# Pooled-key attention feeding a rotated token mix: scores scaled in the copied keys, the row maximum stored with its sign turned, and a newly drawn order of work

## The chip, the cores and the metric

The kernel runs on one core of one Trainium2 chip. The metric is device microseconds of one execution; before and after are compared by the medians of several runs. The engines are called PE (matrix multiplication; PEld is its weight load), DVE (vector), ACT (scalar, activation functions), POOL (GpSimd) and SP (the queue that issues most transfers).

## The reference, cut to what matters

```
def _attn_ref(q, k, v):                      # q, k, v: 8 x 8 x 576 x 64
    scale = 1.0 / np.sqrt(D)                 # D = 64
    k_p = k.reshape(B, H, Sp, pool, D).mean(axis=3)      # pool = 8, Sp = 72
    v_p = v.reshape(B, H, Sp, pool, D).mean(axis=3)
    scores = scale * np.matmul(q, k_p.transpose(0, 1, 3, 2))
    scores = scores - np.max(scores, axis=-1, keepdims=True)
    attn = np.exp(scores)
    attn = attn / (np.sum(attn, axis=-1, keepdims=True) + 1e-09)
    return np.matmul(attn, v_p)

def _moe_ref(x, w_theta, w_tok_r, w_tok_i, w_ch):        # x: 8 x 576 x 512
    theta = x @ w_theta
    zr = x * np.cos(theta)
    zi = x * np.sin(theta)
    y = np.einsum('ts,bsd->btd', w_tok_r, zr) + np.einsum('ts,bsd->btd', w_tok_i, zi)
    u = x + y
    return u + np.maximum(u @ w_ch, 0.0)
```

The attention output, with its heads side by side, is the x of the second part. The four weights arrive as 64-bit numbers and are turned into pairs of 32-bit words in the kernel.

## The kernel before, in words

The work goes over eight batches b. For each batch there are streams of small steps, and every stream is a Python generator that issues the instructions of one step each time it is called:

- k, v and Q load keys, values and queries (SP). K sums eight neighbouring keys (the pooling) and puts them, transposed on PE, into the block tile kpT; V does the sums of the values.
- S{b}.{m} is the softmax of one of five token tiles (the function soften): four groups of matmuls of kpT with the queries into PSUM (line 648), the maximum of 72 scores for each of eight heads on DVE (tile mx, line 682), eight exponentials with a sum each on ACT (line 691, tile e_eps), one instruction that adds the small constant to the sums (line 695), the reciprocal on DVE (line 707), and two steps that multiply by it (lines 712 to 723). For batches from 2 on, a DVE transpose into G follows (line 732), and E moves blocks of G by 16 transfers into eraw. Between the maximum and the exponentials one short ACT instruction (line 687) multiplies the maximum by minus the score scale, because the exponential takes scale times score plus a bias.
- X multiplies the weights by the pooled values, T rotates by cosine and sine (pt, line 829; g, lines 835 to 858), Z and Y split z into two parts whose sum keeps the accuracy of 32 bits, and M is the token mix (py, line 972), U splits u, and F is the final product (pf, line 1075). The weights come by h (theta), w and W (token weights, turned on PE) and c (channel weights); P and R make sums of the turned token weights.

The order of all this is written out by hand of a program: SCHEDULE is a text of 2166 words. A word such as S1.2a calls the next step of stream S1.2 and says that a step that can run on several engines runs on ACT (a), DVE (v) or POOL (g). All engines' queues follow this one order; SP's transfers too. A step's engine and its place are thus fixed when the kernel is built, and an engine that waits for one instruction holds up all that stands behind it in its queue.

In batch 0 the maximum, the multiplication and the exponentials are three words; from batch 1 on the maximum and the multiplication are one word, so the short ACT instruction stands in ACT's queue at the place of the maximum. The score scale is 1/(8 * sqrt(64)) = 1/64 in every softmax (the factor 1/8 is the mean over eight keys).

Of the kernel before, what the change touches and what calls it, by code (L numbers as in the profile page):

```python
# [82 lines left out]
T3.3 T3.3 F2.3.1 F2.0.1 S4.3 F1.2.1 F2.1.1 F2.2.1 Z3.0a F2.1.0 v5.1 Z3.0v Z3.0g Z3.0g S4.4 V5.1g F2.0.0 F2.0.1 F2.0.1
Z3.0v M3.0 M3.0 F2.2.1 Z3.0a Z3.0v Q5.1 M3.0 F2.1.1 Q5.1 Z3.0g S4.4 S4.4a F2.0.1 Q5.1 M3.0 M3.0 Z3.0g Z3.0v S4.4v
Z3.0a X4.0 F2.2.1 Y3.0g M3.0 S4.4 M3.0 Z3.0v F2.3.1 F2.1.1 Z3.0g M3.0 F2.2.0 Z3.0a Y3.0v Z3.0g F2.3.0 M3.0 F2.3.1
Z3.0v Z3.1v Y3.0g X4.0a M3.0 Z3.0g M3.0 X4.0a S5.2 Z3.1v Z3.1a k6.2 M3.1 k6.0 M3.0 S5.4 Z3.0g T4.0a M3.0 E4.2 S5.2
S5.2 E4.2 S5.3 Y3.1g Z3.1v T4.0v Z3.1v F2.2.1 Y3.1g K6.0v S5.2 Z3.1a M3.1 S5.2a S5.4 Y3.1v M3.1 E4.2 E4.2 Z3.1v Z3.1g
M3.1 S5.3 U3.0.0a T4.0 M3.1 S5.2v U3.1.0g Z3.1g k6.1 M3.0 Z3.1v Z3.1a Z3.1v M3.1 M3.1 S5.2 S5.3 S5.3 Y3.1v T4.0 T4.0
# [58 lines left out]
def tile_attn_moe(  # L147
# [485 lines left out]
    def soften(b, m):  # L633
# [47 lines left out]
        for scv, mxv, _, _ in views:  # L681
            nc.vector.tensor_reduce(mxv, scv, AX.X, ALU.max)  # L682
# [583 lines left out]
```

## Time and profile before

| what | value |
|---|---|
| median of 3 runs | 562.45 us (561.65 to 563.61) |
| the profiled execution | 562.28 us |
| span of its profile | 560.5 us |
| granted clock of PE, mean | 0.985 |
| busy: PE, PEld, DVE, ACT, POOL | 524.5, 477.6, 475.1, 408.5, 326.8 us |

The span runs from the first to the last instruction; 1.8 us of the profiled execution's time lie around it. Matmuls overlap in their pipeline, so that the busy time of PE is more than the time for which it holds up the next matmul.

### The profile page before, as it was taken

Reading aid. Unit: us, or ns where it says so; the run is one execution under the profiler, and the core shown is the slowest. Engines: PE = TensorE matmul, PEld = TensorE weight load, DVE = VectorE, ACT = ScalarE, POOL = GpSimd, SP = SyncE. Lnnn points to the kernel's source line nnn. Section 1 sums busy time; section 2 is a strip of 40 time slices with the busy share of each in tenths; the row PEclk is TensorE's granted clock in tenths of the full one; section 3 lists DMA queues with packets and bytes.
Section 4 is the critical chain, followed back from the end, with each engine's and each line's share of the span. In section 5 each row is a group of like instructions: output and inputs, shape, how many; then the busy total and the mean of one; then the engine's idle time right before and its main releaser. Section 6 shows DMA issues by size and latency. Waiting matters only on the chain.

```text
span 560.5 us, 11892 instructions
## 1 busy us (share of the span) xinstructions
PE 524.5 (94%) x3927; PEld 477.6 (85%) x3927; DVE 475.1 (85%) x913; ACT 408.5 (73%) x1318; POOL 326.8 (58%) x458
## 2 busy tenths in 40 slices
PE   6687679999999999999999999999999999999996
PEld 6575468898998899889989888989999888889996
DVE  3996999987999888998899979897997879977864
ACT  2896899897898789889757767876987758644211
POOL 4543574365596767765486647567767546534451
PEclk9989987999999999999999999999999999999999
DMA  9999410273667867554845657345436461220126
GB/s 264 319 221 229 109 38 1 69 149 93 118 114 129 131 151 131 125 107 80 146 96 93 103 100 129 71 79 117 70 57 102 87 112 22 34 37 1 23 44 105
DMA packets 232493, 58.92 MB, mean 105 GB/s; under 512 B 218864, under 2 KB 220528, under 8 KB 232432
## 3 DMA queue, kind: packets, MB, share of 16 engines
q1 hardware_dynamic: 227456, 57.52, 51.3%
q10 hardware_dynamic: 4976, 0.64, 0.8%
q8 instruction: 31, 0.51, 0.4%
q14 instruction: 30, 0.25, 0.2%
HBM read 38.86 MB, written 9.44 MB: 86 GB/s over the span
## 4 chain that ended last, share of the span: by engine, by line
PE 57%; DVE 16%; ACT 12%; DMA 7%; issue 3%; POOL 2%; SPq 2%; DVEq 0%; ACTq 0%; POOLq 0%
PE py L972 22%; PE pf L1075 11%; PE pt L829 11%; ACT e_eps L691 5%; PE s L648 4%; PE pv L778 2%; DMA qst<-in_q_dram 2%; PE px L843 2%; DVE mx L682 1%; DMA kprst<-in_k_dram 1%; DMA kpst<-in_k_dram 1%; PE pv L785 1%; DVE xT L988 1%; PE kpp L542 1%; ACT en L712 1%
## 5 line engine op out<-in xcount | busy, mean ns | idle before, releaser
L972 PE MATMUL py<-WTh,zs 128*128 128x288 f32 x576 | 96.1, 292 | 0.2 <-DVE g L837 0.2
L691 ACT ACTIVATE e_eps<-s,mx 128x72 f32<-128x72 f32 (+1 forms) x304 | 92.7, 328 | 2.8 <-DVE en L716 1.5
L972 PEld LDWEIGHTS py<-WTh,zs 128*128 128x128 f32 x576 | 79.8, 189 | 5.4 <-issue 2.5
L691 ACT ACTIVATION_READ_ACCUMULATOR e_eps<-s,mx 128x1 f32 (+1 forms) x304 | 64.9, 214 | 0.0
L988 DVE TENSOR_TENSOR xT<-py,xT 128x288 f32<-128x288 f32 x106 | 46.8, 446 | 18.9 <-PE py L972 18.9
L890 DVE TENSOR_TENSOR zs<-z,zs 128x512 fp32r<-128x512 f32 x80 | 60.9, 767 | 1.6 <-POOL zs L208 0.6
L191 POOL TENSOR_TENSOR zs<-z,zs 128x256 fp32r<-128x256 f32 x52 | 41.6, 823 | 24.1 <-ACT zs L206 12.8
L972 PE MATMUL py<-WSh,zs 128*128 128x288 f32 x336 | 54.1, 290 | 1.3 <-DVE xT L988 0.6
L206 ACT CAST zs<-z 128x512 fp32r<-128x512 f32 x56 | 34.0, 615 | 25.9 <-POOL z L191 12.0
L648 PE MATMUL s<-kpT,qT 128*128 128x144 f32 (+1 forms) x320 | 48.6, 298 | 3.3 <-DVE qT L208 1.4
L712 ACT ACTIVATE en<-e_eps,ri 128x64 f32<-128x64 f32 (+1 forms) x176 | 44.6, 337 | 6.0 <-DVE G L732 3.1
L972 PEld LDWEIGHTS py<-WSh,zs 128*128 128x128 f32 x336 | 46.0, 189 | 3.0 <-DVE zs L890 1.1
L648 PEld LDWEIGHTS s<-kpT,qT 128*128 128x128 f32 (+1 forms) x320 | 42.5, 185 | 6.7 <-DVE qT L208 1.7
L191 POOL TENSOR_TENSOR z<-z 128x256 f32<-128x256 f32 (+1 forms) x58 | 42.2, 747 | 9.9 <-DVE zs L890 7.2
L972 PE MATMUL py<-WTl,zs 128*128 128x288 f32 x288 | 47.1, 286 | 0.0
L1075 PE MATMUL pf<-uh,chh 128*128 128x288 f32 x256 | 44.0, 293 | 1.8 <-DVE uh L208 1.4
L829 PE MATMUL pt<-th,xh 128*128 128x512 f32 x148 | 41.9, 407 | 1.6 <-DVE zo L864 0.6
L191 POOL TENSOR_TENSOR ul<-xT,uh 128x288 fp32r<-128x288 f32 x37 | 31.5, 861 | 20.0 <-ACT uh L206 14.1
L835 ACT ACTIVATE g<-pt,c_magic 128x512 f32<-128x512 f32 x35 | 23.9, 683 | 25.1 <-PE pt L829 13.2
L1075 PE MATMUL pf<-ul,chh 128*128 128x288 f32 x256 | 41.9, 286 | 0.0
L1075 PE MATMUL pf<-uh,chl 128*128 128x288 f32 x256 | 41.8, 286 | 0.0
L972 PEld LDWEIGHTS py<-WTl,zs 128*128 128x128 f32 x288 | 40.1, 189 | 0.0
(238 smaller groups left out, 1445.3 us busy)
## 6 DMA issues: line engine op xcount, KB each, us to landing
out_dram<-R SPq DMA_DIRECT2D x112, 72.0 KB
kpst<-in_k_dram SPq DMA_DIRECT2D x15, 512.0 KB
vpst<-in_v_dram SPq DMA_DIRECT2D x28, 256.0 KB
qsst<-in_q_dram SPq DMA_DIRECT2D x96, 72.0 KB
eraw<-G SPq DMA_DIRECT2D x96, 60.0 KB
eraw<-G SPq DMA_DIRECT2D x96, 40.0 KB
WTh_st<-in_moe_w_theta_dram SPq DMA_DIRECT2D x4, 512.0 KB
wcraw<-in_moe_w_ch_dram SPq DMA_DIRECT2D x4, 512.0 KB
```

Source lines behind the costliest of these rows:

```text
L191: nc.gpsimd.tensor_tensor(out[:, r], a[:, r], b[:, r], op)
L206: nc.scalar.copy(out, src)
L648: nc.tensor.matmul(scs[c // 2][:n, 2 * SP * (c % 2) : 2 * SP * (c % 2 + 1)], qT[:, c, t0 : t0 + n], kpT[:, c, :], start=True, stop=True,)
L691: nc.scalar.activation(e[:n, x], scs[j][:n, SP * y : SP * y + SP], AF.Exp, bias=mx[:n, x : x + 1], scale=scale, accum_out=sm[:n, x : x + 1],)
L712: nc.scalar.activation(en[:n, GM * h : GM * h + GM], e[:n, h, 0:GM], AF.Copy, scale=ri[:n, h : h + 1])
L778: nc.tensor.matmul(pvs[j][to : to + 64, c, :gn], vm[r, 2 * j + c, :], ev[r, 2 * j + c, :gn], start=True, stop=False,)
L829: nc.tensor.matmul(as_written(pt), l[:, c, :], by_turns(r[:, c, :]), start=i == 0, stop=i == 11)
L835: nc.scalar.activation(halves(g), in_order(pt), AF.Identity, bias=c_magic)
L890: ENG[pick()].tensor_tensor(dst[:, 1], src, f32(dst[:, 0]), ALU.subtract)
L972: nc.tensor.matmul(as_written(to[:, 0 : S // 2]), left(l, kk), by_turns(weights(what, kk)[r]), start=start and i == 0, stop=stop and i == ...
L988: nc.vector.tensor_tensor(halves(u), in_order(py[:, 0 : S // 2]), halves(u), ALU.add)
L1075: nc.tensor.matmul(as_written(pv[:, :n]), l[:, kk, o], by_turns(uhl[r][:, kk]), start=i == 0, stop=i == 11,)
```

## The change: what it does

The pooled keys are multiplied by 1/64 while they are copied into kpT (four copies and one remainder for each batch), by an activation on ACT or a multiplication on DVE in place of a plain copy. The scores in PSUM are then scaled already. The maximum is stored with its sign turned by the reducing instruction itself, so that it is the bias of the exponential as it is. The ACT instruction of line 687 is gone (40 times, 5 words of batch 0 with it), and the exponentials take no scale. The order is drawn anew: SCHEDULE has 2161 words, nearly all streams' words stand at other places (half of them within 6 places of their old one, the farthest 130), and 308 words name another engine.

```diff
+    def scaled(e, out, src, by):
+        if e == "a":
+            nc.scalar.activation(out, src, AF.Copy, scale=by)
+        else:
+            ENG[e].tensor_scalar(out, src, by, None, ALU.mult)
+
+    SCORE = 1.0 / (POOL * math.sqrt(D))
...
-        copy(e, blocks[0:64, :, 0::3], heads[:, 0::2].rearrange("p (j c) g -> p j c g", c=2))
+        scaled(e, blocks[0:64, :, 0::3], heads[:, 0::2].rearrange("p (j c) g -> p j c g", c=2), SCORE)
...
-        copy(pick(), kpT[64:128, 3, GR:SP], pr[0:64, 0:64])
+        scaled(pick(), kpT[64:128, 3, GR:SP], pr[0:64, 0:64], SCORE)
...
-            nc.vector.tensor_reduce(mxv, scv, AX.X, ALU.max)
+            nc.vector.tensor_reduce(mxv, scv, AX.X, ALU.max, negate=True)
         if b == 0:
             yield
         sm = work([P, 8], F32, "sm", f"sm{b}_{m}", bufs=2)
         if b < SUMS_ON_ACT:
-            nc.scalar.mul(mx[:n], mx[:n], -scale)
-            yield
+            if b:
+                yield
             for x in range(8):
                 j, y = at(x)
                 nc.scalar.activation(
                     e[:n, x], scs[j][:n, SP * y : SP * y + SP], AF.Exp,
-                    bias=mx[:n, x : x + 1], scale=scale, accum_out=sm[:n, x : x + 1],
+                    bias=mx[:n, x : x + 1], accum_out=sm[:n, x : x + 1],
                 )
```

Of the order, the words that load in the first part, before and after:

```
before: k1.0 Q0.3 h3 w1.1 h2 Q0.4 w1.0 Q1.1 k1.1 Q1.0 v0.2 w2.0 v0.1 v1.0 Q1.2 v0.0 k1.2 ... w3.0 Q1.4 c0 k2.2 w4.0 c1
after:  h3 Q0.3 k1.0 Q0.4 h2 Q1.1 w1.0 w1.1 v0.2 k1.1 Q1.0 w2.0 v0.1 v1.0 v0.0 Q1.2 k1.2 ... w3.0 Q1.4 c0 w4.0 k2.2 c1
```

## Rows read from the trace of the kernel before

**Rows 1.** The page, busy time, share of the span and instructions of each engine.
```profile
PE 524.5 (94%) x3927; PEld 477.6 (85%) x3927; DVE 475.1 (85%) x913; ACT 408.5 (73%) x1318; POOL 326.8 (58%) x458
```

**Rows 2.** Stages: length, busy PE, PEld, DVE, ACT, POOL; clock, DMA share, GB/s.
```profile
20.00:55.00 35.00, 25.75 (x181) 21.22 (x179) 29.86 (x59) 30.11 (x120) 15.43 (x17) 0.90 1.05 252
55.00:86.00 31.00, 20.53 (x126) 16.25 (x127) 28.60 (x46) 27.24 (x62) 19.70 (x22) 0.90 0.24 68
...
100.00:460.00 360.00, 355.38 (x2693) 326.10 (x2692) 316.07 (x604) 288.79 (x990) 232.74 (x342) 1.00 0.58 107
```

**Rows 3.** The chain that ended last: start, length, what; four kinds of matmul.
```profile
417.50 1.47 PE py L972 x12
418.97 0.98 PE s L648 x8
421.78 2.59 PE pt L829 x12
444.09 4.41 PE pf L1075 x36
```

**Rows 4.** PE alone in one stage, for tiles py, pf, pt, s in turn.
```profile
100.00:460.00 360.00, 151.16 (x1126) 1.00 0.58 107
...
100.00:460.00 360.00, 76.00 (x574) 1.00 0.58 107
...
100.00:460.00 360.00, 75.71 (x324) 1.00 0.58 107
...
100.00:460.00 360.00, 36.92 (x256) 1.00 0.58 107
```

**Rows 5.** Groups of instructions: the maximum, its multiplication, the copies into kpT.
```profile
L682 DVE TENSOR_REDUCE mx<-s 128x8 f32<-128x576 f32 (+2 forms) x42 | 29.8, 714 | 1.9 <-PE s L648 1.9
...
L687 ACT ACTIVATE mx<-mx 128x8 f32<-128x8 f32 (+1 forms) x40 | 8.2, 205 | 17.1 <-DVE mx L682 16.9
L707 DVE RECIPROCAL ri<-sm 128x8 f32<-128x8 f32 (+1 forms) x40 | 7.6, 190 | 3.8 <-ACT sm L695 3.3
...
L206 ACT COPY kpT<-pk 64x288 f32<-64x288 f32 (+3 forms) x24 | 5.0, 258 | 0.1
```

**Rows 6.** The chain around the multiplication of the maximum.
```profile
134.16 0.22 ACT mx L687
```

**Rows 7.** Waits: who waited for whom, total us, times, longest.
```profile
ACT mx L687 <- DVE mx L682: 16.9, 12, 2.4
```

**Rows 8.** ACT by shape: a scaled copy and a plain one out of PSUM, smaller ones.
```profile
L712 ACT ACTIVATE en<-e_eps,ri 128x64 f32<-128x64 f32 x152 | 38.5, 337 | 4.7 <-DVE G L732 3.1 <-DVE ri L707 1.0 <-PE per L746 0.6
...
L791 ACT ACTIVATE xT<-pv 128x512 f32<-128x512 f32 x13 | 7.5, 592 | 6.2 <-DVE R L1112 3.4 <-PE pv L785 2.7
...
L206 ACT COPY eraw<-pe 128x512 f32<-128x512 f32 x7 | 4.1, 579 | 1.1 <-PE pv L785 0.7 <-PE pe L741 0.4
...
L206 ACT COPY kpT<-pkr 64x64 f32<-64x64 f32 x7 | 1.5, 209 | 0.2
```

**Rows 9.** Groups: the final product with PE's waits before it, and key sums on DVE.
```profile
L1075 PE MATMUL pf<-uh,chh 128*128 128x288 f32 x256 | 44.0, 293 | 1.8 <-DVE uh L208 1.4 <-DVE g L837 0.4
...
L466 DVE TENSOR_TENSOR kpst<-kpst 128x512 f32<-128x512 f32 (+1 forms) x16 | 9.5, 593 | 0.5 <-DMA kpst<-in_k_dram 0.2
```

**Rows 10.** The chain in the start: two transfers, and where PE's long run begins.
```profile
36.63 7.90 DMA kprst<-in_k_dram
46.50 8.84 DMA qst<-in_q_dram
85.77 4.99 PE pt L829 x12
```

**Rows 11.** SP in time: the transfers of c0, k2.2 and w4.0.
```profile
47.97 0.33 SPq L368 DMA_DIRECT2D wcraw<-in_moe_w_ch_dram  x1
55.94 0.49 SPq L494 DMA_DIRECT2D kprst<-in_k_dram  x1
56.48 0.59 SPq L404 DMA_DIRECT2D WSh_st<-in_moe_w_tok_r_dram  x1
```

More of the change, by code (lines that the diff above doesn't have):

```diff
@@ new lines @@
+w0.0 Q0.0a h1 h0 K0 h1v K0a K0.2v w0.1v K0 K0v Q0.1 h3 S0.0 w0.1a Q0.2 Q0.3 w0.1v k1.0 Q0.2a h1 w0.1 h0a S0.0 w0.1
+Q0.4 Q0.1v S0.1 h0v h0v h3v S0.0 h2 h0 Q1.1 Q0.3 Q0.4 S0.1 h3a Q0.3a S0.2 S0.0 w1.0 h3a h0 K1.0v S0.1 h0v Q0.4a w1.1
+v0.2 S0.0v S0.0g h0 h3 k1.1 S0.0 S0.0a S0.3 h2v S0.0 S0.2 S0.1 W0 h2v S0.2 h2v h2 h3 S0.1v h2 S0.4 S0.0v S0.3 S0.2
+w1.0v w1.1a S0.1v w1.0a Q1.0 w1.1a h3v w1.0a h2v Q1.1 Q1.1a K1.1v h2 w2.0 S0.1 S0.2v Q1.0 w1.0 S0.3 w1.1a h3 w1.0
+w2.0a S0.2g Q1.0v v0.1 S0.4 W0a w1.1 V0.2 w1.1 v1.0 S0.1v K1 S0.1 W0 V0.1 W1 V1.0v S0.3 v0.0 S0.2 Q1.2 S0.4 W0 w2.0v
@@ new lines @@
+S0.3g W1a V0.0 W0v S0.4 S0.3g K1a W0 S0.1v W1 k1.2 w2.0a Q1.3 w2.1 V0a W1 W1v V0 Q1.2 W1 w2.1a Q1.3 w2.1a w3.1 v1.1
+X0.0 X0.0a S0.2a w2.0 Q1.3v Q1.2v w3.1a X0.0v S0.3 S0.2 S0.2a S0.4v S0.3a T0.0v S0.4v K1.2g w3.0 w2.1a S0.4 T0.0v
+T0.1a V1.1v S0.3 Q1.4 T0.0 T0.1v c0 S0.4a S0.4 w3.1a w4.0 w3.0a c0v w2.1 S0.3a S0.4a K1 T0.0 w3.0v w2.0 w3.0a c0a T0.0
+w2.1 X0.2 Q1.4 T0.0 K1v c0a c0 T0.0 w3.1v T0.0a w3.0 X0.2v k2.2 X0.2v T0.1 T0.0 T0.1 W2 c1 T0.2a T0.3a K2.2g w4.0a
+w4.0a w3.0 w3.1 W2v S1.0 w4.0v S1.0 W2 c0 T0.1 w3.1 T0.1 v1.2 w4.0 W3 c0g T0.0 S1.0 c0g T0.2v W2 W3v T0.0 T0.1 T0.1a
@@ new lines @@
+Z1.0v U0.3.1a U0.3.1v Z1.0v E2.0 F0.1.1 k3.1 Z1.0a Z1.0v T1.4 F0.1.1 F0.1.1 S2.4 E2.0 T1.4 T1.4 F0.0.1 Z1.0g S2.2
+K3.1v T1.4 S2.2 V3.2g M1.0 F0.0.0 E2.0 S2.3 R2g T1.4 F0.1.1 E2.0 F0.0.1 F0.3.0 F0.2.1 T1.4 Z1.0a F0.3.1 M1.0 S2.2a
+S2.3 F0.2.1 Z1.0g Q3.0 S2.4 Y1.0g F0.3.1 S2.2g F0.0.0 K3 R2g Y1.0g F0.0.1 M1.0 S2.3 M1.0 S2.2 Z1.0g R2a S2.3 Z1.0g
+Z1.0v K3v Y1.0g R2g Q3.1 M1.0 F0.0.1 Z1.0a S2.3a M1.0 Z1.0v S2.3g M1.0 V2g S2.4 Q3.1 Z1.0v R3v F0.3.1 R3v S2.3 R3a
+S2.4 Z1.0g F0.3.1 F0.2.0 M1.0 F0.2.1 M1.0 Z1.0g X2.0 K3 S2.4a Z1.0v R3g S2.4v M1.0 K3a Y1.0a Z1.1g Z1.1g Z1.1a S2.4
@@ new lines @@
+U1.1.0g T2.1 T2.1 U1.0.0g T2.2a S3.0 K4.0g U1.1.0v T2.1 F1.3.0 k4.1 F1.1.0 E3.2 T2.2v M1.1 F0.2.1 V4.2g E3.2 T2.1a
+T2.2 T2.1 F1.3.0 F1.0.0 F1.1.0 T2.1 S3.0 T2.1 T2.2 F1.1.0 Q4.0 K4.1g S3.1 F1.2.0 T2.2 U1.0.1v T2.2 T2.2 T2.2a T2.3g
+F1.2.0 F1.0.0 U1.3.1v U1.0.1v T2.2 T2.2 U1.2.1a U1.3.1g T2.2 T2.3 U1.1.1a T2.3 U1.1.1v S3.0 K4 U1.2.1g T2.3 F1.1.1
+S3.0g v4.0 F1.1.1 Q4.1 F1.0.0 T2.3 F1.1.1 T2.3 V3g T2.3a S3.0g T2.3 T2.3 S3.0 S3.1 F1.0.1 F1.0.1 T2.3 F1.3.1 Q4.1
+Z2.0v F1.0.1 Z2.0v Z2.0v F1.2.1 F1.1.1 K4a F1.2.1 M2.0 Q4.1 F1.0.1 S3.1 V4.0g k5.2 K4 K4a Z2.0v X3.2 F1.2.0 F1.2.1
@@ new lines @@
+U2.0.1a U2.1.1a F2.2.0 T3.3 U2.0.1v T3.3 U2.2.1a U2.1.1v U2.3.1g T3.3 K5a Q5.1 T3.3a U2.2.1v U2.3.1v F2.3.1 T3.3
+F2.1.1 F2.0.0 T3.3 T3.3 Z3.0a F2.1.1 F2.1.1 F2.0.1 Z3.0v Z3.0a F1.3.1 M3.0 V5.1g k6.2 F2.3.1 Z3.0v Z3.0v M3.0 M3.0
+Z3.0v F2.0.1 F2.1.1 Z3.0g F2.2.1 k6.0 F2.0.1 Z3.0g S4.4 Z3.0g F2.0.0 S4.4 S4.3 M3.0 Y3.0v M3.0 F2.2.1 F2.2.0 F2.2.1
+S4.4a Z3.0v X4.0 S4.4g M3.0 Z3.0a S4.4 F2.0.1 F2.3.0 M3.0 Z3.0v Z3.0g Z3.0a F2.3.1 M3.0 M3.0 Q5.1 Z3.0g X4.0a X4.0a
+M3.0 Y3.0a E4.2 U3.0.0a Z3.0g M3.0 Z3.1g S5.2 Z3.0a S5.4 T4.0a T4.1a M3.0 Z3.1v E4.2 E4.2 S5.2 S5.4 Z3.1a Y3.0v Z3.1v
@@ new lines @@
+F4.0.1 V6g F4.2.1 M5.0 S6.2 M5.0 Z5.0g S6.3 Z5.0g S6.3a S6.3g M5.0 F4.0.1 Z5.0v Z5.0g F4.0.1 F4.3.1 M5.0 Z5.0v M5.0
+F4.2.1 M5.0 Q7.1 Z5.0g Z5.0g M5.0 K7 S6.4 M5.0 S6.4 F4.1.1 F4.0.1 S6.3 M5.0 Z5.0g U5.0.0a K7a K7 S6.4a F4.3.0 K7a
+F4.1.0 S6.4v F4.3.1 X6.0 M5.0 S6.4 Z5.0g E6.2 Y5.0g Z5.0g M5.0 Y5.0v Z5.0g X6.0a X6.0a S7.2 Z5.1v E6.2 T6.0a Z5.0v
+Z5.1g S7.4 M5.1 Z5.1a T6.1g S7.2 S7.2 Y5.0g S7.4 E6.2 Z5.1g M5.0 Z5.0v M5.0 M5.1 Z5.1v Y5.1g S7.3 Y5.1v E6.2 T6.0v
+S7.2 Z5.1v M5.1 Z5.1v Z5.1g M5.1 T6.0 U5.2.0a S7.3 M5.0 M5.1 Z5.1v Z5.1v M5.1 S7.2a Y5.1g Z5.1a Z5.1v Z5.1v F4.3.1
@@ new lines @@
+F5.2.1 T6.1 T6.2 T6.2 S7.0 V7v V7.1g T6.2 F5.1.0 T6.2 T6.2 T6.2a F5.3.1 T6.2 F5.1.1 T6.2 F5.3.1 X7.2 F5.1.1 T6.2
+F5.1.1 F5.3.0 F5.3.1 T6.3 S7.0g T6.3 T6.3 X7.2v X7.2a X7.2v S7.0g T6.4v T6.3 T6.3a T6.3 S7.1 T6.3 T6.3 Z6.0a S7.0
+T6.4g Z6.0v Z6.0a T7.3a Z6.0v Z6.0v T6.4 T6.4 M6.0 Z6.0a T6.4 T6.4 Z6.0v M6.0 T6.4 T6.4a T6.4 M6.0 S7.1 S7.1 Z6.0g
+Z6.0g T6.4 Z6.0v Z6.0g M6.0 M6.0 T6.4 Y6.0a Z6.0g M6.0 M6.0 Z6.0g M6.0 S7.1 T7.3v T7.3 Z6.0v Z6.0g Y6.0g S7.1a T7.3
+S7.1v S7.1 Z6.0v E7.0 Z6.0g T7.3 M6.0 M6.0 M6.0 Z6.1a Z6.1v Z6.1a Z6.1v Y6.0g Y6.0a Z6.0v M6.0 M6.0 M6.0 Y6.0v M6.0
@@ new lines @@
+M6.1 M6.0 T7.2a Z6.1v Y6.1a M6.0 Z6.1g Y6.1v E7.0 Z6.1v Z6.1v T7.2v Z6.1g M6.1 M6.1 Z6.1v M6.1 T7.2 M6.1 M6.1 E7.0
+Z6.1a T7.3 Y6.1g Z6.1v Z6.1g M6.1 Z6.1a T7.3 E7.0 Z6.1v Z6.1v U6.0.0a Y6.1g Z6.1v Z6.1g T7.3a M6.1 M6.1 M6.1 T7.3
+Y6.1v T7.3 T7.3 X7.0 X7.0v T7.4a U6.3.0v X7.0a M6.1 T7.2 U6.0.0g T7.0g T7.2 T7.2 T7.2 T7.0g T7.2a T7.0 T7.2 U6.3.0v
+T7.1a T7.2 T7.2 T7.0 U6.1.0a T7.0 T7.0 U6.2.0g T7.1g M6.1 U6.2.0g T7.0 T7.0a U6.1.0g F5.1.1 T7.0 T7.1 T7.0 T7.0 T7.1
+M6.1 F6.2.0 T7.1 T7.1 T7.1 M6.1 T7.1a T7.1 T7.1 Y7.0v T7.1 F6.1.0 F6.3.0 Z7.0a F6.1.0 Z7.0v Z7.0a Z7.0v F6.3.0 Z7.0v
@@ new lines @@
+F6.0.0 U6.3.1v Y7.0g U6.2.1v U6.0.1a U6.1.1a F5.3.1 M7.0 F6.0.0 Z7.0a M7.0 Z7.0v M7.0 Z7.0v M7.0 Y7.0v M7.0 Z7.0v
+Z7.0v M7.0 U6.3.1g Z7.0v Z7.0v Z7.0v U6.2.1v U6.0.1v Y7.0g M7.0 U6.1.1v Z7.0a M7.0 M7.0 M7.0 F6.0.1 Z7.0g Z7.0v M7.0
+F6.1.0 Z7.0a Z7.1v Y7.0g M7.0 Z7.1v Z7.1a F6.3.1 Z7.0g M7.0 F6.2.0 Z7.1g F6.3.1 F6.0.1 Y7.1g M7.0 Z7.1v Z7.1g F6.2.1
+Z7.1v F6.1.1 F6.3.1 M7.1 Z7.1g Z7.1a F6.1.1 Y7.1v M7.1 M7.1 Z7.1v U7.2.0v U7.0.0g M7.1 Y7.1g Z7.1v M7.1 F6.1.1 M7.1
+Z7.1v F6.1.1 Z7.1v U7.1.0g U7.2.0v Z7.1a Z7.1g F6.3.0 Y7.1v M7.1 M7.1 U7.0.0g M7.1 Z7.1g F6.2.1 M7.1 U7.1.0v U7.3.0a
@@ L136 @@
+U7.3.0v M7.1 F7.3.0 Z7.1g F6.2.0 F6.2.1 Y7.1g F7.2.0 F7.1.0 F6.3.1 F7.2.0 F6.0.1 F7.0.0 F7.3.0 Z7.1g M7.1 F7.1.0
+F7.3.0 U7.0.1g U7.0.1v F6.2.1 U7.2.1v F7.2.0 U7.3.1a M7.1 M7.1 U7.1.1v U7.1.1v F7.0.0 F6.0.0 U7.3.1g U7.2.1g F7.3.1
+F7.0.0 F6.0.1 F7.2.0 F7.1.0 F7.3.1 F7.2.1 F7.3.1 F7.0.1 F7.3.1v F7.3.1v F7.2.1 F7.3.0 F7.2.1 F7.1.0 F7.3.1 F7.0.1
+F7.2.1a F7.1.1 F7.2.1a F7.0.1 F7.0.0 F7.1.1 F7.2.1 F7.0.1v F7.1.1 F7.1.1a F7.0.1v F7.1.1v F7.0.1 F7.1.1
 """
@@ L559, in keys @@
         blocks = kpT.rearrange("p (j c) (s g) -> p j (c s) g", c=2, s=2)
-        copy(e, blocks[0:64, :, 0::3], heads[:, 0::2].rearrange("p (j c) g -> p j c g", c=2))
-        copy(e, blocks[64:128, 0, 1:3], heads[:, 1:4:2])
-        copy(e, blocks[64:128, 1, 1], heads[:, 5])
-        copy(e, blocks[64:128, 1, 2, 0:GR], pk[0:64, 3, P - GR :])
+        scaled(e, blocks[0:64, :, 0::3], heads[:, 0::2].rearrange("p (j c) g -> p j c g", c=2), SCORE)
+        scaled(e, blocks[64:128, 0, 1:3], heads[:, 1:4:2], SCORE)
+        scaled(e, blocks[64:128, 1, 1], heads[:, 5], SCORE)
+        scaled(e, blocks[64:128, 1, 2, 0:GR], pk[0:64, 3, P - GR :], SCORE)
         yield
@@ L638, in soften @@
         nt, mi = len(tiles), m - tiles[0]
-        scale = 1.0 / (POOL * math.sqrt(D))
         split = b == 0 and m % 2
@@ L699, in soften @@
                 nc.vector.tensor_tensor(
-                    e_, scv, mxv.unsqueeze(len(shape)).broadcast_to([n, *shape]), ALU.subtract
+                    e_, scv, mxv.unsqueeze(len(shape)).broadcast_to([n, *shape]), ALU.add
                 )
             yield
-            nc.scalar.activation(e[:n], e[:n], AF.Exp, scale=scale)
+            nc.scalar.activation(e[:n], e[:n], AF.Exp)
             yield
```

161 lines of the change are left out of this document (56 added, 105 removed).

## The prediction, made before the changed kernel was run

> **What bounds the kernel now.** I read the page's busy times first, then the stages, then the chain that ended last, and last the waits and groups around the softmax. The reader is to see first that PE is busy for most of the span and that DVE, ACT and POOL all have room on average [rows 1]; an average says nothing of stages, so the table by stage comes next [rows 2]. There are three. Up to some 86 us the kernel starts: weights and the first batches arrive, and between 20 and 55 us all transfer engines are taken (share 1.05). From 55 to 86 us transfers fall to 0.24, but DVE is busy for 28.60 of 31 us and ACT for 27.24: here the conversion of the last weights sets the pace. From 86 us to the end PE runs almost without a pause.
>
> How much PE could still give back must not be read from its busy time, because one matmul's record is longer than its distance from the next. The chain gives the distance: 12 matmuls of py in 1.47 us, 36 of pf in 4.41 us (0.1225 us each), 12 of pt in 2.59 us (0.216 each), 8 of s in 0.98 us [rows 3]. With the counts of the stage from 100 to 460 us that is 1126 x 0.1225 = 137.9, 574 x 0.1225 = 70.3, 324 x 0.216 = 70.0 and 256 x 0.1225 = 31.4 us [rows 3, 4], together 309.6. The other 413 matmuls of the stage (2693 less 2280) are transposes and the small products of pv; at half to the whole of 0.1225 us each they add 25 to 51 us, and I take 0.085, an estimate, and so 35 us. So about 345 of 360 us are real work of PE, and some 15 us are gaps (0 to 25 by the two ends), against 4.6 us by the matmul records [rows 2]. I go by the 15 us. The Trainium skill (Perfetto Trace Analysis, Identifying the Most-Contended Engine) says that matmul busy share is no measure of headroom and that the busy share of weight loads should be taken; by it the gaps of this stage would be 360 - 326.10 = 34 us, and the trace's distances bear out less than half of that.
>
> **What the change removes.** 40 ACT instructions of 205 ns, 8.2 us of ACT busy time, and with them ACT's wait for the maximum at the place of the maximum: 16.9 us of idle time [rows 5]. Neither is on PE. On the chain the multiplication appears in five places in all, with 0.03 to 0.22 us each, 0.66 us together; the longest is [rows 6], and the load of the exponential's table and the exponentials follow it there. I count 0.7 us saved, nearest to the chain's own rows. Below lies 0, if the chain then runs by another way of the same length; above, 12 x 0.205 = 2.5 us, if each of the twelve times that ACT stood waiting here [rows 7] were on the path. The wait itself doesn't vanish: the first exponential now waits for the maximum, and what is late next behind it in ACT's queue is the rest of the eight exponentials and after them DVE's reciprocal, which waited for ACT's sums 3.3 us in all [rows 5]. In batches from 1 on, ACT is free in the meantime for the words between the maximum and the exponentials.
>
> **What it adds.** Of the 8 batches, 7 copy their keys on ACT in the new order (28 instructions and 4 remainders, the other remainders on DVE). No row shows a scaled copy into kpT. From below: a scaled copy out of PSUM of 512 columns took 592 ns and a plain one 579 [rows 8], so 13 ns more, 0.4 us in all. From above: a scaled copy of 64 columns with a scale for each row took 337 ns and a plain copy of 64 columns 209 [rows 8], 128 ns more, 4.1 us in all. I take the first, since it too reads PSUM and has a constant for its scale; it hides behind ACT's idle time (idle for 71 of 360 us in the long stage [rows 2]). Without that cover it is at most 4.1 us, on a chain that crosses the keys in three places only. Turning the sign inside the maximum: nearest rows are the maximum itself, 714 ns, and the shortest DVE instruction of this shape, 190 ns [rows 5]. From below it is 0, from above 40 x 0.19 = 7.6 us of DVE, as if a second instruction ran. I take 0: the instruction still reads 576 and writes 8 columns. Dropping the scale of the exponentials is nothing, as a constant operand goes away.
>
> **The order.** Every word of the two orders was matched and costed by the like rows of the trace. The switch between the tables of exponential and sine comes out equally often: 19 runs of exponentials and 19 of sines in both. Over the whole kernel DVE gains 0.3 us of work, ACT loses 3.6 (8.2 go, the moved words bring 4.8 back), and POOL loses 5.8. No engine becomes a new bound from that.
>
> In the start the sum is less kind. Up to the last split of the token weights, DVE has 1.2 us more to do, ACT 3.0 less and POOL 4.5 less. The largest single piece is the sum of half of batch 1's keys that goes from POOL to DVE: two additions of 593 ns on average [rows 9] and a last one of 0.3, about 1.4 us. In the other direction, transfers stand better: SP issued c0 at 47.97 us and then stood still until 55.94, because k2.2 waited for a buffer behind the transfers of the chain [rows 10, 11]; the last token weights, w4.0, stood behind it. In the new order w4.0 is ahead of k2.2 and can go some 8 us sooner, and v0.2 is ahead of k1.1, which waits for a buffer too. Queued behind these on SP are only loads. DVE was idle for 5.1 us of 20 to 55 us [rows 2]; data that comes sooner can fill at most that. Bounds for the start: +1.2 (nothing comes sooner, DVE sets the pace) and -5.1 + 1.2 = -3.9. I take -0.5, nearer to the upper bound, because w4 was not what DVE waited for once it was busy.
>
> In the long stage I compared distances, as PE work between a step and the step that needs it. Between the split of u (U) and the first final product that reads it, 16 of 64 distances were under 1.5 us, now 3; PE waited 1.8 us there [rows 9]. A load of keys stands 5.5 us ahead of its sum in the median, was 2.2. Between the maximum and the exponentials the mean grows from 3.8 to 4.9 us, but between exponentials and reciprocal it shrinks from 2.8 to 1.9, less than the 2.7 us that the exponentials and the constant take on ACT: DVE can wait there 19 times in place of 13. With 1 us lost on DVE each, 6 us of DVE's 44 idle ones, in part on the path. I take -1.3 us: most of the 1.8 us before pf. Bounds: -15 (all gaps) and +6.
>
> **The sum.** The profiled execution took 562.28 us, 560.5 of span and 1.8 around it, 0.17 below the median. 562.28 - 0.7 - 0.5 - 1.3 = 559.8; with the 0.17 of the median, 560.0 us. A measurement of this kernel can tell a change of about 0.3% from none, 1.7 us here, so the forecast lies just past that.
>
> **The rivals.**
>
> - No change, 562.5 us. ACT has 27% idle time [rows 1], and in the long stage PE's order of work is the same but for shifts of a few words. Then 8 us less on ACT buy nothing. Against it: the five places on the chain, and the gaps before pf. Chance 0.2.
> - Slower: the place is DVE in the start and behind the exponentials. DVE's 1.2 us more delay PE's long run, which began at 85.77 us [rows 10], by as much; and the six more short ways from exponentials to reciprocal cost 1 us of DVE each, half of it on the path: 562.45 + 1.2 + 3 = 566.7 us. It decides from the point where DVE stays without idle time between 40 and 57 us and the reciprocals wait more than some 6 us (3.3 before). For it speaks DVE's 28.60 of 31 us; against it, that less work on ACT gives the sums earlier. Chance 0.28.
> - Much faster: the new order closes half of the gaps in the long stage, 7.5 us, beside 1.2 us from the other two terms: 562.45 - 8.7 = 553.8 us. For it speak the longer ways from loads and from U; against it, that hundreds of moves would have to go the same way. Chance 0.06. If the gaps are those between weight loads, 360 - 326.10 = 33.9 us [rows 2], half of them is 17 us and the time 562.45 - 17 - 1.2 = 544.3 us, with a chance of 0.01. The Trainium skill's rule above (Perfetto Trace Analysis) would have it so.
> - The sign costs DVE an instruction's time: 7.6 us on DVE, a third of it on the path, 565 us. The rows give no sign of it. Chance 0.03, slower.
>
> The forecast itself, 558 to 561.5 us, has 0.42. Some of it lies within 0.3% of before.
>
> **How the numbers follow.** Faster by over 0.3% (below 560.8): 0.42 of the forecast and 0.07 of the two much faster cases, less 0.02 for its near edge, 0.47. Within 0.3%: the rival with no change and the near edge, 0.22. Slower: 0.31. Cases of both signs hold most of the chance; the likeliest one's own range is 558 to 561.5 us. The 8-in-10 range leaves out a part of the much faster cases and the upper end of the slower ones, whose bounds reach 1.2 + 6 = 7.2 us above 562.45: 552.5 to 568 us.
>
> **What would show it.** Right: no row for line 687; ACT's wait for the maximum stands at line 691; the group of 40 maxima keeps some 714 ns; kpT's rows on ACT read ACTIVATE with 260 to 280 ns; PE's long run begins between 84 and 87 us; the idle time of PE before pf falls under 1 us. Wrong: the reciprocal's wait above 6 us or the long run beginning after 88 us (slower), or a stage from 100 to 460 us whose work ends 5 us sooner or later, since the order could do either and its hundreds of small moves are only costed here in sums.

## The result, and the profile after

| | median us | lowest to highest | runs |
|---|---|---|---|
| before | 562.45 | 560.63 to 563.61 | 7 |
| changed | 567.63 | 564.33 to 568.34 | 7 |

The ratio is 1.0077, 95% interval 1.0050 to 1.0103: slower by 0.8%, where the prediction had 560.0 us. The profiled execution of the changed kernel took 564.33 us (span 562.5), the fastest of its seven; what follows about the start has to be read with that in mind.

The page, its busy times (against [rows 1]):

```profile
PE 528.2 (94%) x3927; PEld 482.2 (86%) x3927; DVE 474.9 (84%) x915; ACT 407.6 (72%) x1278; POOL 315.6 (56%) x449
```

The forty instructions are gone from ACT, whose busy time hardly moved; POOL lost 11 us; PE became busier, with the same 3927 matmuls, at a mean granted clock of 0.974 against 0.985. So some of them took longer. The groups by line, columns as in [rows 5, 9]:

```profile
L1081 PE MATMUL pf<-uh,chh 128*128 128x288 f32 x256 | 44.4, 296 | 4.0 <-ACT kpT L212 3.2 <-DVE uh L208 0.8
...
L688 DVE TENSOR_REDUCE mx<-s 128x8 f32<-128x576 f32 (+2 forms) x42 | 29.7, 714 | 5.7 <-PE s L654 5.7
...
L713 DVE RECIPROCAL ri<-sm 128x8 f32<-128x8 f32 (+1 forms) x40 | 7.6, 190 | 1.5 <-ACT sm L701 1.4
...
L212 ACT ACTIVATE kpT<-pk 64x288 f32<-64x288 f32 (+3 forms) x28 | 6.0, 264 | 1.0 <-PE s L654 0.9
```

The maximum with its sign turned takes 714 ns, as before. A scaled copy into kpT takes 264 ns where the plain one took 258. The new thing is in the first row: PE stood 3.2 us before the final product, waiting for ACT's copies of keys. The waits show that it is one single wait (total, times, longest):

```profile
ACT e_eps L697 <- DVE mx L688: 5.1, 5, 1.4
...
PE pf L1081 <- ACT kpT L212: 3.2, 1, 3.2
...
DVE ri L713 <- ACT sm L701: 1.4, 4, 0.5
```

The chain of work around it:

```profile
211.96 2.61 PE pt L835 x12
...
214.59 0.70 ACT g L841
...
217.36 0.72 ACT g L864
...
218.10 1.28 ACT L697
...
219.40 2.54 ACT e_eps L697 x16
...
221.96 0.30 ACT sm L701
...
222.26 0.29 ACT kpT L212
...
222.57 0.47 ACT kpT L212 x3
...
223.08 3.17 PE pf L1081 x12
226.25 1.47 PE py L978 x12
```

Read it backwards. The twelve matmuls of a final product (word F1.2.1) begin at 223.08 us, when the last of ACT's four copies into kpT ends. These copies (word K4a) empty the PSUM bank that holds the transposed keys of batch 4. F1.2.1 reads nothing of kpT or of these keys, and yet it waits for the copies: so it must be writing into the same bank. PE's timeline has the transposed keys, the last matmuls before the wait, and the wait (in brackets, with what ended it):

```profile
214.39 0.60 PE L561 MATMUL pk<-ident,kp 128*64 128x128 f32 x4
...
219.19 0.65 PE L1081 MATMUL pf<-ul,chh 128*128 128x288 f32 x4
223.08 1.33 PE L1081 MATMUL pf<-uh,chh 128*128 128x288 f32 x4 [3.24 <-ACT kpT L212]
```

PE had transposed the keys at 214.39 us; the copies came 8 us later because in ACT's queue they stand behind the rotation of tile T2.3, the load of the exponential's table (1.28 us), eight exponentials with the reading of a sum behind each (sixteen instructions, 2.54 us) and their closing one (0.30 us). The order itself turned the two words round: F1.2.1's product stands two words ahead of K4a in the changed order, and stood 22 words behind it in the order before. In the kernel before, ACT's timeline has the copies ahead of all that, behind the first step of the same rotation only (start, length, what):

```profile
215.11 0.69 ACT L835 ACTIVATE g<-pt,c_magic 128x512 f32<-128x512 f32 x1 [1.15 <-DVE z L869]
215.69 0.84 ACT L206 COPY kpT<-pk 64x288 f32<-64x288 f32 x4
216.56 0.63 ACT L850 ACTIVATE sn<-g 128x512 f32<-128x512 f32 x1
```

And the wait is not the whole price: the product that follows took 3.17 us in the chain, where twelve such matmuls are 1.47 us [rows 3]. Stretches of the changed kernel around the wait (columns as in [rows 2]; PEclk is the granted clock):

```profile
210.00:219.00 9.00, 9.00 (x68) 8.60 (x67) 7.33 (x17) 7.15 (x11) 6.49 (x11) 1.00 0.82 148
219.80:223.00 3.20, 0.04 (x1) 0.00 (x0) 1.89 (x5) 3.16 (x20) 1.51 (x2) 0.94 0.81 123
223.05:226.05 3.00, 2.97 (x12) 2.97 (x13) 0.00 (x0) 0.00 (x0) 2.02 (x3) 0.50 0.73 160
226.10:236.00 9.90, 9.90 (x84) 8.39 (x84) 8.59 (x17) 6.34 (x23) 4.17 (x6) 1.00 0.38 73
```

By the end of 3.2 us without a matmul the clock had fallen from 1.00 to 0.50 (2.4 to 1.2 GHz); it stayed there for the twelve matmuls of F1.2.1, and was back at 1.00 with the next product. 3.24 us of idle time and 1.5 us of slow matmuls (3.00 less 1.47) make 4.8 us.

### The profile page after: what moved, and what is told of

The parts are those of the page before. It is cut to its first block, busy times and chain, and to the rows that moved or that the text cites. A ratio compares the mean times of both kernels' runs of the same rounds, so it can differ in the third digit from the quotient of the medians.

```text
span 562.5 us, 11824 instructions
## 1 busy us (share of the span) xinstructions
PE 528.2 (94%) x3927; PEld 482.2 (86%) x3927; DVE 474.9 (84%) x915; ACT 407.6 (72%) x1278; POOL 315.6 (56%) x449
## 4 chain that ended last, share of the span: by engine, by line
PE 73%; DVE 9%; ACT 8%; DMA 6%; issue 2%; SPq 1%; POOL 0%; ACTq 0%; DVEq 0%
PE py L978 29%; PE pt L835 16%; PE pf L1081 15%; PE s L654 5%; ACT e_eps L697 2%; PE px L849 2%; PE pv L784 2%; DMA wcraw<-in_moe_w_ch_dram 2%; DMA kpst<-in_k_dram 2%; PE pv L791 1%; DVE zs L896 1%; DMA kprst<-in_k_dram 1%; DMA out_dram<-R 1%; DVE G L738 1%; DMA out_dram<-rz 1%
## 5 line engine op out<-in xcount | busy, mean ns | idle before, releaser
L191 POOL TENSOR_TENSOR zs<-z,zs 128x256 fp32r<-128x256 f32 x64 | 50.7, 814 | 24.7 <-ACT zs L206 13.6
L896 DVE TENSOR_TENSOR zs<-z,zs 128x512 fp32r<-128x512 f32 x74 | 58.7, 801 | 2.1 <-POOL zs L208 1.0
L654 PE MATMUL s<-kpT,qT 128*128 128x144 f32 (+1 forms) x320 | 47.3, 294 | 2.8 <-DVE qT L208 1.0
L718 ACT ACTIVATE en<-e_eps,ri 128x64 f32<-128x64 f32 (+1 forms) x168 | 42.4, 336 | 5.9 <-DVE ri L713 3.9
L1081 PEld LDWEIGHTS pf<-uh,chh 128*128 128x128 f32 x256 | 36.6, 191 | 5.7 <-ACT kpT L212 3.5
L1088 DVE SCALAR_TENSOR_TENSOR xT<-pf,xT 128x288 f32<-128x288 f32 x64 | 27.9, 443 | 14.9 <-PE pf L1081 14.6
```

Source lines behind the costliest of these rows:

```text
L191: nc.gpsimd.tensor_tensor(out[:, r], a[:, r], b[:, r], op)
L654: nc.tensor.matmul(scs[c // 2][:n, 2 * SP * (c % 2) : 2 * SP * (c % 2 + 1)], qT[:, c, t0 : t0 + n], kpT[:, c, :], start=True, stop=True,)
L718: nc.scalar.activation(en[:n, GM * h : GM * h + GM], e[:n, h, 0:GM], AF.Copy, scale=ri[:n, h : h + 1])
L896: ENG[pick()].tensor_tensor(dst[:, 1], src, f32(dst[:, 0]), ALU.subtract)
L1081: nc.tensor.matmul(as_written(pv[:, :n]), l[:, kk, o], by_turns(uhl[r][:, kk]), start=i == 0, stop=i == 11,)
L1088: nc.vector.scalar_tensor_tensor(halves(oT), in_order(pv[:, :n]), 0.0, halves(oT), ALU.max, ALU.add)
```

## The experiments

Two measures stand beside each other below: the ratio of all runs to those of the kernel before on the same chip, and, from each profile, the stretch from the first matmul of T0.4's product pt, where PE's long run begins, to the end of the span. The second turned out to be sharper (run 9 tests it), but it isn't free of the clock: in nine of the eleven profiles the first four matmuls of the stretch took 2.04 or 2.05 us, at half the clock, and in runs 4 and 6 1.14 and 1.10 us, at the full one. Differences well under 1 us in this column should not be leaned on.

| kernel | T0.4's pt begins, us | span, us | stretch, us | median, us | ratio to before (interval) |
|---|---|---|---|---|---|
| before | 85.77 | 560.5 | 474.7 | 562.45 | |
| before again (e9) | 87.30 | 561.7 | 474.4 | 563.46 (one run) | |
| changed | 83.81 | 562.5 | 478.7 | 567.63 | 1.0077 (1.0050 to 1.0103) |
| changed again (e1) | 83.04 | 561.5 | 478.5 | 566.28 | 1.0080 (1.0054 to 1.0106) |
| keys first (e2) | 85.52 | 559.2 | 473.7 | 561.81 | 0.9998 (0.9977 to 1.0018) |
| old order (e3) | 85.52 | 559.4 | 473.9 | 561.92 | 1.0008 (0.9993 to 1.0024) |
| old code (e4) | 88.31 | 582.6 | 494.3 | 582.35 | 1.0362 (1.0334 to 1.0390) |
| multiplication late (e5) | 87.21 | 566.3 | 479.1 | 570.35 | 1.0121 (1.0071 to 1.0171) |
| c0 later (e6) | 84.35 | 558.2 | 473.8 | 562.52 | 1.0002 (0.9974 to 1.0030) |
| c0 and X2.2 later (e7) | 85.53 | 559.8 | 474.3 | 560.92 | 0.9963 (0.9935 to 0.9990) |
| two orders (e8) | 84.53 | 557.7 | 473.2 | 560.79 | 0.9976 (0.9957 to 0.9995) |

My theory for the first four runs was that the one wait at 223 us is the loss; the rival was that the new order or the new code loses in many small places.

**1. The changed kernel again (e1).** No edit.

> The changed kernel once more, without an edit. Theory A (the order): in the first trace PE stood 3.24 us at 219.8 us before a final product, because its PSUM bank was still held by the keys of batch 4, whose copy into kpT (word K4a) stands in ACT's queue behind a table load and sixteen exponential instructions; the twelve matmuls after it took 3.0 us where 1.47 is usual. This is fixed by the order, so it must be there again within 1 us, and the time is 564 to 568 us. Theory B (the code: the wait for the maximum now at the exponentials, scaled copies): the same time, but the loss is spread over many waits, and the long one is not there each time.

Measured: 566.28 us, and the same single wait of 3.2 us at the same word. Theory A holds: the loss is in the program, and repeats.

**2. Keys first (e2).** The changed kernel with one word of the order moved up 19 places, to where it stood in the old order, ahead of the sine of T2.3's rotation:

```diff
-F1.1.1 T2.3 V3g T2.3a S3.0g
+F1.1.1 K4a T2.3 V3g T2.3a S3.0g
...
-F1.2.1 F1.1.1 K4a F1.2.1 M2.0
+F1.2.1 F1.1.1 F1.2.1 M2.0
```

> The changed kernel with one word moved: the copy of batch 4's keys (K4a) stands before the sine of T2.3, as it did in the order of before, and so ahead of the table load and the exponentials. Theory A: the 3.24 us and the 1.5 us of slow matmuls behind them go, 4.8 us less than e1, and ratio to before 0.998 to 1.002. Theory B: at most 1 us less than e1.

Measured: 561.81 us, ratio 0.9998, and the stretch is 4.8 to 5.0 us shorter than that of the changed kernel. The chain around the place now stays on PE, with three products in a row at full pace:

```profile
216.22 0.44 PE pk L561 x4
216.66 1.47 PE pf L1081 x12
218.13 0.44 PE px L849 x4
218.57 4.41 PE pf L1081 x36
222.98 1.47 PE py L978 x12
```

One word of 2161 carried the loss, and without it the ratio shows no change either way.

**3. The old order (e3).** The new code with the order of before, less the five words of batch 0's multiplication (the third word of S0.0 to S0.4); the first line of each:

```diff
-k0.1 w0.0 K0.1 h1 D Q0.0 w0.0a k0.0 k0.2 w0.1 w0.0v Q0.0 h1v h1v K0.0 h1v Q0.1 h1 w0.0a K0.2 w0.0 Q0.2 K0.0v K0.1a
+k0.1 h1 w0.0 w0.0v w0.0a Q0.0 h1v k0.0 h1v K0.1 w0.0a w0.0 h1v h1 D w0.1 k0.2 K0.1a w0.1v Q0.0 K0.0 K0.0a K0 K0.2
...
```

> The changed code with the order of before (its words without the five of batch 0's multiplication). Theory A: no slower than before, 560 to 562.5 us, ratio 0.996 to 1.000, because only the code's 0.7 us on the chain are left. Theory B: as slow as the changed kernel, 565 us or more, ratio 1.005 or more.

Measured: 561.92 us, ratio 1.0008, interval 0.9993 to 1.0024: theory A's time, with a ratio just above its range, and not theory B. The stretch is 473.9 us against 474.4 and 474.7 of before: the code itself may save 0.5 to 0.8 us there, too little for the ratio to show, and not far from the 0.35 us by which the two profiles of before differ. 8 us less work on ACT bought nearly nothing; that PE sets the pace of the stretch (some 345 of 360 us of work, by the prediction's estimate) fits it.

**4. The old code in the new order (e4).** Copies, maximum and exponentials as before; the multiplication stands, from batch 1 on, in the word of the maximum:

```diff
-        scaled(e, blocks[64:128, 1, 1], heads[:, 5], SCORE)
+        copy(e, blocks[64:128, 1, 1], heads[:, 5])
...
-            nc.vector.tensor_reduce(mxv, scv, AX.X, ALU.max, negate=True)
+            nc.vector.tensor_reduce(mxv, scv, AX.X, ALU.max)
...
+            nc.scalar.mul(mx[:n], mx[:n], -scale)
             if b:
                 yield
```

> The code of before with the new order: the multiplication of the maximum stands at the place of the maximum (in batch 0 at the place of the exponentials), the keys are copied without a scale. Theory A: as slow as the changed kernel or up to 1.5 us slower, 566 to 569 us, ratio 1.006 to 1.012, with the same long wait. Theory B: as fast as before, ratio 0.998 to 1.003.

Measured: 582.35 us, 16 us more than the changed kernel on the same chip. Neither theory had foreseen that. The waits name a place, and the long wait of the changed kernel is there too:

```profile
ACT mx L694 <- DVE mx L689: 39.5, 25, 4.3
...
DVE ri L715 <- ACT sm L703: 9.4, 12, 1.9
...
PE pf L1083 <- ACT kpT L206: 3.3, 1, 3.3
```

ACT stood 39.5 us for the maximum, against 16.9 us in the old order [rows 7]. The new order sets maxima with no regard to when DVE gets to them, and an ACT instruction at that place holds up all of ACT behind it. That is a reading; the next run tests it. The last row shows something else: PE's wait for K4a stands in the new order with the old code as well, and run 3 has the new code without it. So it belongs to the order and not to the code.

**5. The multiplication late (e5).** As run 4, with the multiplication one word later, directly ahead of the exponentials:

```diff
-            nc.scalar.mul(mx[:n], mx[:n], -scale)
             if b:
                 yield
+            nc.scalar.mul(mx[:n], mx[:n], -scale)
             for x in range(8):
```

> The code of before in the new order once more, but with the multiplication of the maximum directly ahead of the exponentials in every batch, not at the place of the maximum. Theory: the 20 us that the old code loses in the new order are ACT's waits for DVE at the place of the maximum, because the new order sets maxima where DVE is late; moved behind them, the same 40 instructions cost next to nothing, and the time is that of the changed kernel plus 0 to 3 us: 566 to 570 us, ratio 1.007 to 1.016, with ACT's wait for the maximum under 8 us. Rival: the 40 instructions themselves (8.2 us of ACT) and the plain copies make ACT too slow for the new order wherever they stand: 575 to 583 us, ratio over 1.024.

Measured: 570.35 us, ratio 1.0121: the ratio is in the theory's range, and the time and ACT's wait lie at its edges (570 us, 8 us).

```profile
ACT mx L696 <- DVE mx L689: 8.0, 8, 1.7
```

The same forty instructions, still 8 us of ACT, and 12 us less of time. In the stretch this run is 0.6 us longer than the changed kernel (479.1 against 478.5), where run 4 was 15.8. The 0.6 is not the whole price of the forty: PE waits for K4a here too, but its clock stays at 1.00, and the 1.5 us of slow matmuls don't follow (the wait in PE's timeline, then stretches in and behind it, columns as in [rows 2]):

```profile
228.12 0.76 PE L1083 MATMUL pf<-uh,chh 128*128 128x288 f32 x4 [3.37 <-ACT kpT L206]
```

```profile
224.75:228.05 3.30, 0.00 (x0) 0.00 (x0) 1.85 (x5) 3.26 (x21) 1.61 (x3) 1.00 0.86 131
228.10:231.10 3.00, 2.98 (x24) 2.99 (x24) 1.21 (x2) 0.00 (x0) 1.89 (x3) 1.00 0.67 142
```

Like for like the forty cost some 2 us there (an estimate: 0.6 and the missing 1.5). So run 4 lost its time to ACT's waits at the place of the maximum, and neither to the work of the instructions nor to the plain copies, which both runs have. The median is 3 to 4 us above the changed kernel's, more than the stretch explains: in the profile PE's long run begins 3.4 to 4.2 us later than in the changed kernel's two. The six runs lie between 566.3 and 575.6 us, and what this program does in the start was not followed up.

**6. c0 later (e6).** Run 2 with three words of the channel weights moved down, because DVE stood 1.8 us at the first of them until its transfer had landed:

```diff
-c0 S0.4a S0.4 w3.1a w4.0 w3.0a c0v w2.1 S0.3a S0.4a K1 T0.0 w3.0v w2.0 w3.0a c0a T0.0 w2.1 X0.2 Q1.4 T0.0 K1v c0a c0
+c0 S0.4a S0.4 w3.1a w4.0 w3.0a w2.1 S0.3a S0.4a K1 T0.0 w3.0v w2.0 w3.0a T0.0 w2.1 X0.2 Q1.4 T0.0 K1v c0v c0a c0a c0
```

> The version with the keys' copies at their early place, and with the first three steps on the channel weights c0 (words c0v, c0a, c0a) 8 to 17 words later, next to the fourth. Theory: in the start DVE stands 1.8 us at c0v until the transfer has landed (57.9 us), with work for 1.9 us behind it that is ready; DVE sets the pace there, so 0.5 to 1.8 us are gained: ratio 0.9965 to 0.999 against before. Rival: what lands last in the start sets the pace, not DVE's queue: no gain, ratio 0.9985 to 1.0015.

Measured: ratio 1.0002, the rival's value; the interval (0.9974 to 1.0030) is too wide to rule out the lower gains of the theory's range (0.9974 to 0.999). In run 2 the chain of the start goes through the transfer of c0,

```profile
46.13 11.64 DMA wcraw<-in_moe_w_ch_dram
```

and in this run it goes through another one, which had landed by 47.72 us, ten us before c0 in run 2 (57.77), from there through PE and DVE, and later through another transfer of channel weights:

```profile
41.25 6.47 DMA chl_st<-in_moe_w_tok_i_dram
...
76.23 3.38 DMA wcraw<-in_moe_w_ch_dram
```

So DVE no longer stands for c0. The long run begins 1.2 us earlier than in run 2 (84.35 against 85.52 us), within the spread of one order's start (run 9 and the last section), and its first matmuls run at full clock. PE then waits for DVE and ACT:

```profile
84.35 1.10 PE L835 MATMUL pt<-th,xh 128*128 128x512 f32 x4
...
88.60 0.30 PE L752 MATMUL per<-ident,en 128*128 128x128 f32 x1 [1.42 <-DVE z L875]
89.77 0.76 PE L978 MATMUL py<-WTh,zs 128*128 128x288 f32 x4 [0.86 <-ACT zs L206]
```

What the clock gave there was lost again in these waits; the stretch is that of run 2 (473.8 against 473.7 us). Whether what lands last sets the pace, as the rival says, stays open.

**7. c0 and X2.2 later (e7).** Run 6 with the first word of X2.2 moved behind the next step of the token mix, since PE's weight load had waited 1.3 us there in run 6 (0.75 us by the matmuls' own rows):

```diff
-T2.1 X2.2 U1.0.0a T2.0 k4.0 M1.1 S3.3
+T2.1 U1.0.0a T2.0 k4.0 M1.1 X2.2 S3.3
```

> As the run before, and with the product of the weights with the values X2.2 one step of the token mix (12 to 15 matmuls, 1.5 to 1.8 us) later, because PE waited 1.3 us there for the exponentials to free its PSUM banks. Theory: PE is what the long stage lacks, so a gap closed on PE is gained in full: 1.3 us less than the run before, ratio 0.994 to 0.997. Rival: the gap moves to the step that follows (its copies, the rotation): the same time as the run before.

Measured: ratio 0.9963, in the theory's range, but the profile doesn't bear the theory out. The stretch is not shorter (474.3 us against 473.8), and PE's timeline shows that the wait moved to the next step, which needs the banks that X2.2 had filled:

```profile
197.36 1.31 PE L784 MATMUL pv<-eraw,vp 64*64 64x320 f32 x16
198.60 0.82 PE L791 MATMUL pv<-eraw,Vr 32*128 32x320 f32 x8
200.22 1.25 PE L654 MATMUL s<-kpT,qT 128*128 128x144 f32 x8 [0.81 <-ACT xT L797]
```

So what there is in the ratio, whose interval overlaps that of run 6, would have to come from the start, whose words are those of run 6; that is not shown. Inconclusive; I don't count it as a gain.

**8. Two orders (e8).** The new code; the old order up to the first product of the token mix (339 words), from there the words that are left, in the order of run 2. Its beginning against that of run 2:

```diff
-k0.1 w0.0 K0.1 h1 D Q0.0 w0.0a k0.0 k0.2 w0.1 w0.0v Q0.0 h1v h1v K0.0 h1v Q0.1 h1 w0.0a K0.2 w0.0 Q0.2 K0.0v K0.1a
+k0.1 h1 w0.0 w0.0v w0.0a Q0.0 h1v k0.0 h1v K0.1 w0.0a w0.0 h1v h1 D w0.1 k0.2 K0.1a w0.1v Q0.0 K0.0 K0.0a K0 K0.2
...
```

> The new code with the old order up to the first product of the token mix (339 words, without the five of the multiplication), and from there the new order with the keys' copies at their early place. Theory: from PE's long run to the end the new order needs 1.05 us less than the old one (473.68 against 474.73 us in the profiles) and its start costs some 1.2 us more, which is why the version with the early copies came out equal; the old start with the new rest then gains 0.5 to 2 us: ratio 0.9965 to 0.999, and 473.4 to 474.2 us from the start of T0.4's product to the end. Rival: the two starts are the same but for the spread of single runs: ratio 0.998 to 1.0005 by the rest alone. A second rival: the cut leaves words of the start out of place, and the gain is lost in a new wait: ratio over 1.0005.

Measured: 560.79 us, ratio 0.9976, interval 0.9957 to 0.9995, and a stretch of 473.2 us, a little under the forecast. This is the fastest of the kernels whose gain the profile bears out. 474.55 (the mean of the two profiles of before) less 473.2 are 1.3 us, and the median is 1.0 us lower: the stretch explains it alone, so the first rival fits as well (0.998 lies in the interval), and that the old start is better is not shown. A gain of 0.24% is also below the 0.3% from which the prediction counted a difference.

**9. The kernel before again (e9).** No edit, one profile.

> The kernel before once more, for one profile. Theory: from the start of T0.4's product (85.77 us) to the end, one order always takes the same time, 474.7 us within 0.2, and what differs from run to run lies before it: the beginning of that product between 83 and 88 us. Rival: the spread arises all along the run: that stretch differs by more than 0.5 us.

The two rows of PE's timeline, of before again and of the changed kernel again:

```profile
87.30 2.04 PE L829 MATMUL pt<-th,xh 128*128 128x512 f32 x4 [0.34 <-ACT eraw L206]
```

```profile
83.04 2.04 PE L835 MATMUL pt<-th,xh 128*128 128x512 f32 x4
```

The stretch came out 0.35 us apart (474.73 and 474.38), a little more than the 0.2 us that I had expected and under the rival's 0.5; for the changed kernel it was 0.15 (478.66 and 478.51). The beginning differs by 1.5 us between the two profiles of before, and by 0.8 us between those of the changed kernel. So in both pairs most of the difference lies in the first 88 us.

## Why the prediction was wrong, by its own steps

**The failed step: "In the long stage I compared distances", -1.3 us.** The stretch after the start became 4.0 us longer (478.6 against 474.55 us, means of two profiles each). The runs split it: the code gives about 0.7 back (run 3), all other moves of the new order 0.2 (473.7 against 473.9, runs 2 and 3), and the one word K4a costs 4.8 to 5.0 (changed kernel and run 2). Only the last stands clear of the 0.35 us by which two profiles of one kernel differ. I had compared means and counts of distances: U to final product, load to sum, maximum to exponentials, exponentials to reciprocal. The distance that decided was on no list: from the transposed keys to the copies that free their bank. And counted as a mean over eight batches it would not have shown: from K to its first copies the mean is 13.0 words before and 12.8 after, and batch 4 alone has the wait. What makes it bad isn't its length in words either (30 against 21) but what stands in between in ACT's queue, a table load and a softmax, and that the product F1.2.1, which takes the bank, stands ahead of the copies. The prediction had costed these copies only by their length, 0.4 us off the path, and had called the keys a place that the chain crosses three times only.

**What that step got right.** The wait for U did fall: without the keys' 3.2 us, PE's idle time before that line is 0.8 us (4.0 less 3.2, and 0.8 in run 2), against 1.8 [rows 9]. I had named "under 1 us" as the sign, and it was buried under a wait of another origin in the same row. Of the signs that I had named for being wrong, the one that came is that of the stage from 100 to 460 us, 5 us sooner or later: the stretch is 4.0 us longer.

**The multiplication, -0.7.** Not contradicted, and too small to be told: 0.5 to 0.8 us in the stretch (run 3), ratio 1.0008. ACT's wait for the maximum fell with it, from 16.9 us at the multiplication to 5.1 us at the exponentials.

**Sign and copies, 0 and 0.4 us off the path.** Right: the maximum takes 714 ns as before, and a copy 6 ns more where 13 were taken. The exponentials without their scale take 329 ns, with it 328.

**The reciprocals.** I feared up to 6 us of new waits on DVE. They fell from 3.3 to 1.4 us.

**The engines' work.** I had DVE gain 0.3 us, ACT lose 3.6 (the parts named there, 8.2 and 4.8, give 3.4) and POOL lose 5.8. In the page DVE lost 0.2, ACT 0.9 and POOL 11.2. None of that carries the result.

**The start, -0.5 with bounds +1.2 and -3.9.** In the two profiles of the changed kernel the long run began 2.0 and 2.7 us earlier than in the first one of before (83.81 and 83.04 us, ahead of the 84 to 87 that I had named as a sign), but these were the fastest of their runs. Run 2, with the same words up to there, began at 85.52 us. The spread of one order covers what I wanted to measure. Whether the new start gains or loses stays open within the 2.5 us by which that one start varied.

**The rivals.** "Slower" came true with a price close to its 566.7 us, but not by its mechanism: the reciprocals waited less, and the start is not shown to be later. That the price is close is luck, as it is that 567.63 us lies just inside the 8-in-10 range (552.5 to 568 us), whose upper end was built from DVE's start and the reciprocals. "No change" is what the ratio shows of the change without the one word (run 2). For the weight-load rule of the Trainium skill (Perfetto Trace Analysis, Identifying the Most-Contended Engine) the gaps of the stage would now be 360 less 323.60, some 36 us; three orders that differ in hundreds of places (runs 2, 3 and 8) lie within 0.7 us of each other in the stretch, which gives no sign of so much room.

```profile
100.00:460.00 360.00, 352.37 (x2658) 323.60 (x2657) 314.80 (x593) 286.21 (x959) 224.82 (x331) 1.00 0.56 105
```

Against [rows 2], that row also shows the one wait from a distance: 35 matmuls fewer fit into the same 360 us.

## What to carry to other kernels

When an order of work is drawn anew, list for each PSUM bank what stands in the queue of the engine that empties it, between the matmul and the copy; a table load and the exponentials behind it make a copy late by more than any mean of distances shows. Check also that the copy still stands ahead of the next product that takes the bank. An instruction that is taken off an engine with room gains nothing by itself, but the place that it had may matter a lot: at the place of the maximum the same 8 us of ACT cost 15.8 us in the new order, ahead of the exponentials some 2. And a change of a few tenths of a per cent is better read from a stretch of the profile behind the noisy start, which repeated within 0.15 to 0.35 us of 474 here, than from medians that need a dozen runs to come within 0.2%; but see that the clock was the same in the places that are compared.

## What the runs showed of the hardware that was not expected

- PE's granted clock fell to half by the end of a single wait of 3.2 us in an else dense run, and stayed there for the next 3.0 us, so that a wait of 3.24 us cost 4.8 (changed kernel, and again in run 1). But the same wait doesn't always cost the same. In run 5 it was longer, 3.37 us, and the clock stayed at 1.00 (rows there). In run 4 it was 3.3 us, and the clock stayed at half for 25 matmuls, 5.6 us where 25 x 0.1225 = 3.1 are usual. What decides between these isn't shown by the runs. The two stretches behind the wait in run 4:

```profile
237.25:240.25 3.00, 2.97 (x12) 2.97 (x13) 0.00 (x0) 0.00 (x0) 2.04 (x3) 0.50 0.67 161
240.25:242.85 2.60, 2.60 (x13) 2.60 (x12) 2.29 (x4) 0.00 (x0) 0.37 (x1) 0.50 0.44 112
```

- A program's beginning varies much more than the rest: PE's long run began at 83.04 to 85.52 us with one and the same start (changed, changed again, run 2), while the stretch behind it repeated within 0.15 us (changed) and 0.35 us (before). Part of the difference shows at one transfer, that of c0: in run 2 it was issued at 46.13 us and landed 11.64 us later (run 6 shows the row), in the changed kernel it was issued at 46.55 us and landed 1.1 us earlier all the same:

```profile
46.55 10.14 DMA wcraw<-in_moe_w_ch_dram
```
